# The last three pairs of token tiles: another order of block products for the last pair, and one store DMA per result tile

## The chip, the cores and the metric

The kernel runs on one core of a Trainium2 chip. The core has five engines with a queue of instructions each: TensorE (PE: matrix products, with weight loads beside them), VectorE (DVE), ScalarE (ACT), GpSimd (POOL) and SyncE (SP), which here only issues DMAs. SBUF is the on-chip memory of 128 partitions, PSUM the 128-partition accumulation memory that products are written to. Sixteen DMA engines move data between SBUF and the chip's main memory; they serve queues that SP, ACT and POOL fill. The metric is the device time of one execution in microseconds (us), as the median of several.

## The reference

Attention with normalised queries and keys, then a two-layer network with a PReLU between the layers:

```python
q_n, k_n = rmsnorm(q, g_q), rmsnorm(k, g_k)          # (8, 12, 448, 64)
attn = softmax(q_n @ k_n.T / 8)
x = (attn @ v).transpose(0, 2, 1, 3).reshape(3584, 768)
h = x @ w_in                                         # 768 -> 2048
g = maximum(h, 0) + alpha * minimum(h, 0)
out = g @ w_out                                      # 2048 -> 768, (3584, 768) float32
```

The change concerns only the last line, for the last of the 3584 tokens, and the way in which its results leave the chip.

## The kernel before

The eight batches of 448 tokens are worked through one after the other, attention first, then the two layers. Which product stands where on TensorE is planned in the kernel's text (lists of bursts, gaps and costs), under a manual schedule; the change touches nothing of that plan. Two batches share one buffer of activations, gT: 16 blocks of 128 hidden units by 896 tokens. The 896 tokens are seven tiles of 128.

For most tiles the second layer is `down` (line 500): 16 products of 128 x 384 into one PSUM bank, a copy to an SBUF tile `osb`, and two stores of 64 rows (line 528). The last two batches (b0 = 6) end otherwise. Tile 0 goes through `down`; tiles 1 to 6 go as three pairs (1, 2), (3, 4), (5, 6) through `quad` (line 576), the last work of the kernel. `quad` sees the pair's activations as a 2 x 2 matrix of blocks (tile by half of the 2048 hidden units), and w_out as another (half of the hidden units by half of the 768 columns, OH = 384). It forms the four result blocks with seven block products instead of eight. The sums of blocks that this needs are made beforehand by POOL: `mix_weights` for the weights, `mix` (lines 559 to 566) for the activations, s1 to s4.

Each product is eight matmuls of 128 x 384 (`product`, line 600). In the order of the code: m1 into bank x; m6 into y; m5 into p; m7 into z; m2 added in PSUM onto x; m4 added onto z; m3 added onto p. ACT copies m1 out of x (line 616) and later the finished x (line 627); VectorE forms u2 = y + m1 (619), u3 = z + u2 (624), and the results p + u3 (631), z + u2 (635) and, after m3, p + u2 (640). In the last pair (`last`) m5 and m3 are each split into two halves of 192 columns in banks of their own, so that the final addition and its store go in two pieces.

The banks: x and p are one two-bank tile `oq` (pool pss), y and z a second one; the middle pair takes y and z from the pool psa (`oqa`, one buffer) and x and p from psf (`oqm`, two buffers). The last pair takes its two half-banks for m5 and m3 from psf, so that its own p is not used.

The results go into tiles `osb` of 128 tokens x 384 columns, of which there are four buffers: a new result waits until the store of the one four before it has landed. `send` (line 568) issues the stores. The output is addressed as `out4`, batch, j (0 to 6), 64 rows, 768 columns, where token = row x 7 + j: a tile of 128 tokens is two values of j with 64 rows each, and consecutive rows of one j lie 7 x 768 numbers apart in memory. So a tile is stored by two DMAs of 64 rows of 1536 bytes, both from SP's queue; the two halves of the last result (640) put one of their two DMAs on ACT's queue. In the three pairs that makes 24 DMAs on SP and two on ACT. SP does its issues in order; each waits for the instruction that wrote its source and for the last DMA that used its semaphore.

Of the kernel before, what the change touches and what calls it, by code (L numbers as in the profile page):

```python
# [9 lines left out]
FP32 = mybir.dt.float32  # L10
# [11 lines left out]
def kernel(  # L22
# [12 lines left out]
    nc = tc.nc  # L35
# [4 lines left out]
    J = S // 64  # L40
# [4 lines left out]
    OH = DM // 2  # L45
# [14 lines left out]
    psa = ctx.enter_context(tc.tile_pool(name="psa", bufs=1, space=bass.MemoryType.PSUM))  # L60
# [8 lines left out]
    out4 = out.rearrange("(b p j) m -> b j p m", b=B, j=J)  # L69
# [486 lines left out]
    def block(t, f):  # L556
        return gT[:, ts(f, HF), ts(t, 128)]
# [8 lines left out]
        nc.gpsimd.tensor_sub(out=g[:, 3], in0=block(t, 1), in1=g[:, 1])  # L566

    def send(b0, t, oh, o, c=slice(0, None), split=False):
        for half in range(2):
            bb, j = divmod(2 * t + half, J)  # L570
            dst = out4[b0 + bb, j, :, ts(oh, OH)]
            (nc.scalar if split and half else nc.sync).dma_start(
                out=dst[:, c], in_=o[ds(64 * half, 64), c]
            )

    def quad(b0, t, wide, last=False):

        s1, s2, s3, s4 = (mixes[t][:, n] for n in range(4))
        if wide:
            even, odd = (  # L580
                pss.tile([128, 2, 512], FP32, name="oq", tag="sc") for _ in range(2)
            )
            x, p = even[:, 0], even[:, 1]
        else:
            odd = psa.tile([128, 2, 512], FP32, name="oqa", tag="acc")
            x, p = (psf.tile([128, 512], FP32, name="oqm", tag="mm") for _ in range(2))
        y, z = odd[:, 0], odd[:, 1]
        full = (slice(0, OH),)
        ps = [p]
        if last:  # L590
            full = (slice(0, OH // 2), slice(OH // 2, OH))
            ps = [psf.tile([128, 512], FP32, name="oqm", tag="mm") for _ in range(2)]

        def whole(f, m):
            return lambda ft: w_out_sb[:, HF * f + ft, ts(m, OH)]

        def mixed(n):
            return lambda ft: tw[n, ft // QF][:, ft % QF]

        def product(bank, g, v, first, c=slice(0, OH)):  # L600
            for ft in range(HF):
                nc.tensor.matmul(  # L602
                    out=bank[:, c], lhsT=g[:, ft], rhs=v(ft)[:, c],
                    start=(first and ft == 0), stop=(ft == HF - 1),
                    skip_group_check=True,
                )

        def part(name):
            return ld.tile([128, OH], FP32, name=name, tag="qs", bufs=4)

        def result():
            return ffn.tile([128, OH], FP32, name="osb", tag="osb", bufs=4)

        product(x, block(t, 0), whole(0, 0), True)
        m1 = part("m1")
        nc.scalar.copy(out=m1, in_=x[:, :OH])
        product(y, s2, mixed(1), True)
        u2 = part("u2")
        nc.vector.tensor_add(out=u2, in0=y[:, :OH], in1=m1)
        for b, c in zip(ps, full):  # L620
            product(b, s1, mixed(0), True, c)
        product(z, s3, mixed(2), True)
        u3 = part("u3")
        nc.vector.tensor_add(out=u3, in0=z[:, :OH], in1=u2)
        product(x, block(t, 1), whole(1, 0), False)
        o = result()
        nc.scalar.copy(out=o, in_=x[:, :OH])
        send(b0, t, 0, o)
        o = result()
        for b, c in zip(ps, full):  # L630
            nc.vector.tensor_add(out=o[:, c], in0=b[:, c], in1=u3[:, c])
        send(b0, t + 1, 1, o)
        product(z, block(t + 1, 1), mixed(3), False)
        o = result()
        nc.vector.tensor_add(out=o, in0=z[:, :OH], in1=u2)
        send(b0, t + 1, 0, o)
        o = result()
        for b, c in zip(ps, full):
            product(b, s4, whole(1, 1), False, c)
            nc.vector.tensor_add(out=o[:, c], in0=b[:, c], in1=u2[:, c])  # L640
            send(b0, t, 1, o, c, last)

    def spin(count, wide=True):

# [11 lines left out]
    den_at, av_at, split = {}, {}, {}  # L656
# [5 lines left out]
    while m < NG * J or steps:  # L662
# [21 lines left out]
        while len(bursts[n]) < limit and m < NG * J:  # L684
            y, j = divmod(m, J)
# [91 lines left out]
    for b in range(B - 1):  # L777
# [9 lines left out]
        for n in range(lo, hi):  # L787
            clock += cost(n)
            free = True
            while ups or old or new:  # L790
                two = n in dens and pre(dens[n]) and len(gaps[n]) < 2
                if old and (not ups or (free or two) and (
                    wide(n) or len(old) > sum(wide(c) for c in range(n, hi))
                )):
                    u = old.pop(0)
                elif ups:
                    u = ups.pop(0)
                else:
                    u = new.pop(0)
# [31 lines left out]
    for n, g in enumerate((g_q, g_k)):  # L831
        for h in range(2):
            nc.gpsimd.dma_start(
                out=rows[NF + n : NF + n + 1, ds(64 * h, 64)], in_=g.unsqueeze(0)
# [9 lines left out]
    both, full, lo, hi = slice(0, 2), slice(0, J), slice(0, K0), slice(K0, J)  # L844
    for h in range(2):
        part_square("q", slice(h, h + 1), full, nc.scalar)
    for h in range(2):
# [13 lines left out]
        out=gain, in0=cols[:, NF : NF + 1], in1=cols[:, NF + 1 : NF + 2]  # L861
# [31 lines left out]
    for n in range(NB):  # L893
# [61 lines left out]
        if n in roots:  # L955
            y = roots[n]
# [41 lines left out]
        for k, (f, a) in enumerate(gaps[n]):  # L998
# [3 lines left out]
            else:  # L1002
                f(*a, spare)
                done += 1
                if n in jobs and not (lead and done < 5) and (
                    n < av_at[2 * G - 1] or done % 2
                ):
                    g, c = jobs[n].pop(0)
# [3 lines left out]
                while late and done == late[0][0]:  # L1012
                    _, g, c = late.pop(0)
# [19 lines left out]
    for t in (1, 3, 5):  # L1033
        quad(B - 2, t, t != 3, t == 5)
# [30 lines left out]
```

## Time and profile before

| | us |
|---|---|
| Median of three runs | 426.13 (425.56 to 426.2) |
| The profiled execution, its own time | 425.32 |
| Its span, first to last instruction | 423.6 |
| TensorE busy | 410.0 (97%) |
| Last result written by VectorE (417.83 + 0.36) | 418.19 |
| SP's last eight issues | 415.75 to 420.97 |

The page gives, for each engine, its busy time and its share of the span; the chain that ended last is followed back from the last instruction. A line of a timeline gives start, duration, engine, line of the kernel, operation, and the tile written and read (out<-in); in square brackets the idle time of the engine before it and what ended it. SPq and ACTq are the queues on which these engines issue DMAs: the duration there is that of issuing, and the time from the issue to the landing of the data stands in the answer by source line. A DMA view counts packets (here one per row of 1536 bytes, plus packets of 4 bytes that set the semaphores) and gives the time they took as a share of 16 engines' time in the window. Over the whole span TensorE is busy 97%, and it is the chain's main part (83%).

### The profile page before, as it was taken

To read this page: it belongs to the slowest core of one execution; us is meant where nothing else is said; L and a number is where in the kernel's file an instruction comes from. 1 tells how busy PE (TensorE), PEld (TensorE's weight loads), DVE (VectorE), ACT (ScalarE), POOL (GpSimd) and SP (SyncE) were. 2 spreads that over 40 slices of the span, in tenths; PEclk is the share of its full clock that TensorE was granted. 3 is DMA by queue.
4 is the path that set the end of the run, shared out by engine and by line. 5 is a ranking of instruction groups with operands and counts; after the bars stand their busy time and mean duration, and the time that the engine had idled before them with its cause. 6 is when DMAs were issued, how large, how long until landed. Compare 5 with 4: busy or idle time off the path is not lost.

```text
span 423.6 us, 11137 instructions
## 1 busy us (share of the span) xinstructions
PE 410.0 (97%) x4731; PEld 214.3 (51%) x4731; DVE 224.4 (53%) x335; ACT 278.4 (66%) x390; POOL 290.1 (68%) x201
## 2 busy tenths in 40 slices
PE   8789999999999999999999999999999999999994
PEld 3344454544455454544555445554555545555663
DVE  3875964556464636636565454557463353355232
ACT  5898887778856686668846677667856577255100
POOL 6689994494996289382993569572982999940960
PEclk9999999999999999999999999999999999999998
DMA  8999999999638975568456974547225501100233
GB/s 192 239 244 226 211 192 201 232 163 243 121 82 124 197 126 127 86 135 182 80 117 111 174 177 107 101 85 150 46 44 100 118 2 22 39 19 2 56 85 85
DMA packets 68530, 53.37 MB, mean 126 GB/s; under 512 B 35568, under 2 KB 68480, under 8 KB 68480
## 3 DMA queue, kind: packets, MB, share of 16 engines
q1 hardware_dynamic: 53760, 39.83, 43.0%
q0 software_dynamic: 13984, 11.81, 18.7%
q10 hardware_dynamic: 736, 1.02, 1.0%
q8 instruction: 37, 0.61, 0.6%
q14 instruction: 13, 0.11, 0.1%
HBM read 45.62 MB, written 11.01 MB: 134 GB/s over the span
## 4 chain that ended last, share of the span: by engine, by line
PE 83%; ACT 6%; POOL 4%; DVE 4%; issue 1%; ACTq 1%; POOLq 0%
PE op L508 23%; PE hT L454 21%; PE hTa L454 8%; PE sc L329 8%; PE av L368 5%; PE opa L508 4%; PE oq L602 4%; PE dn L368 3%; ACT expT L343 3%; POOL rden L356 2%; PE avb L368 2%; PE oqm L602 2%; ACT ah L494 2%; PE dnb L389 2%; DVE gT L498 1%
## 5 line engine op out<-in xcount | busy, mean ns | idle before, releaser
L343 ACT ACTIVATE expT<-sc,expb 128x896 f16<-128x896 f32 x168 | 161.3, 1003 | 42.5 <-PE sc L329 42.2
L179 POOL TENSOR_TENSOR qs<-nat,rr 128x896 f16<-128x896 f32 x41 | 68.4, 1690 | 81.8 <-issue 39.3
L454 PE MATMUL hT<-xT,w_in_sb 128*128 128x448 f16 x558 | 115.7, 353 | 0.8 <-DVE gT L498 0.5
L454 PEld LDWEIGHTS <-w_in_sb 128*128 128x128 f16 x768 | 73.2, 98 | 74.0 <-issue 9.4
L508 PE MATMUL op<-w_out_sb,gT 128*128 128x384 f16 x592 | 101.4, 326 | 0.5 <-DVE gT L498 0.5
L508 PEld LDWEIGHTS <-gT 128*128 128x128 f16 x704 | 66.1, 98 | 53.0 <-issue 11.8
L494 ACT ACTIVATE ah<-hT,cols 128x448 f16<-128x448 f32 x92 | 58.1, 632 | 41.8 <-PE hT L454 40.9
L498 DVE TENSOR_TENSOR gT<-hT,ah 128x448 f16<-128x448 f32 x93 | 57.8, 623 | 49.2 <-ACT ah L494 48.4
L155 POOL TENSOR_TENSOR sq<-nat 128x896 f32<-128x896 f32 (+1 forms) x47 | 75.4, 1625 | 8.2 <-DMA nat<-in_q_dram 8.0
L356 POOL TENSOR_TENSOR rden<-rden,expT 128x896 f32<-128x896 f32 x30 | 56.8, 1894 | 2.4
L329 PE MATMUL sc<-qT,kT 64*32 64x448 f16 (+1 forms) x1092 | 53.9, 356 | 4.4 <-ACT expT L343 2.2
L163 DVE TENSOR_REDUCE ss<-sq 128x14 f32<-128x896 f32 (+1 forms) x48 | 48.9, 1038 | 1.5 <-POOL sq L155 1.3
L520 DVE COPY osb<-op 128x384 f32<-128x384 f32 x37 | 20.5, 555 | 54.4 <-PE op L508 54.0
L454 PE MATMUL hTa<-xT,w_in_sb 128*128 128x448 f16 x198 | 42.8, 352 | 0.0
L329 PEld LDWEIGHTS <-kT 64*32 64x32 f16 (+1 forms) x1092 | 16.9, 93 | 35.6 <-issue 29.0
L494 ACT ACTIVATE ah<-hTa,cols 128x448 f16<-128x448 f32 x33 | 20.9, 634 | 15.3 <-PE hTa L454 15.2
L498 DVE TENSOR_TENSOR gT<-hTa,ah 128x448 f16<-128x448 f32 x33 | 20.6, 623 | 17.6 <-ACT ah L494 17.0
L439 DVE TENSOR_TENSOR xT<-av,rden 128x896 f16<-128x896 f32 x16 | 17.5, 1091 | 21.4 <-ACT rden L410 15.4
L368 PEld LDWEIGHTS <-vt 64*32 64x32 f16 (+1 forms) x1260 | 21.4, 94 | 12.7 <-issue 2.5
L368 PE MATMUL av<-expT,vt 64*32 64x448 f16 (+1 forms) x812 | 26.2, 349 | 0.0
L508 PE MATMUL opa<-w_out_sb,gT 128*128 128x384 f16 x112 | 19.4, 327 | 0.0
L563 POOL TENSOR_TENSOR gs<-gT 128x1024 f16<-128x1024 f16 x3 | 6.4, 2117 | 16.6 <-DVE gT L498 16.6
(98 smaller groups left out, 330.5 us busy)
## 6 DMA issues: line engine op xcount, KB each, us to landing
out_dram<-osb SPq DMA_DIRECT2D x110, 96.0 KB, 2.2
nat<-in_q_dram SPq DMA_DIRECT2D x46, 224.0 KB, 4.3
nat<-in_k_dram SPq DMA_DIRECT2D x46, 224.0 KB, 4.6
vt<-in_v_dram POOLq DMA_DIRECT2D x16, 336.0 KB, 6.1
w_in_sb<-in_moe_w_in_dram POOLq DMA_DIRECT2D x12, 256.0 KB, 7.4
w_out_sb<-in_moe_w_out_dram POOLq DMA_DIRECT2D x4, 768.0 KB, 11.3
nat<-in_q_dram ACTq DMA_DIRECT2D x2, 224.0 KB, 4.9
nat<-in_k_dram ACTq DMA_DIRECT2D x2, 224.0 KB, 6.4
```

Source lines behind the costliest of these rows:

```text
L155: nc.gpsimd.tensor_mul(out=sqf[:, c], in0=src[:, c], in1=src[:, c])
L163: nc.vector.tensor_reduce(out=o[:, c], in_=sqs[y, nm][:, c], axis=AXIS_X, op=ALU.add)
L179: eng.tensor_mul(out=t.rearrange("p j h d -> p h j d"), in0=nat[y, nm], in1=rr_t[y][:, "qk".index(nm)].unsqueeze(3).broadcast_to((128, 2, ...
L329: nc.tensor.matmul(out=sc[ds(64 * g + m * c, m), par, :S].rearrange("p (j c) -> p j c", j=J), lhsT=kT[ds(64 * par, 64), j, g, ts(c, m)], r ...
L343: nc.scalar.activation(out=expT[y][:, j], in_=scs[y, j][:, :, :S], func=AF.Exp, scale=QK_SCALE, bias=expb[:, 0:1],)
L356: nc.gpsimd.tensor_add(out=s, in0=e[:, 0] if j == 1 else s, in1=e[:, j])
L368: nc.tensor.matmul(out=accs[g][ds(m * h, m), :S], lhsT=weights(g, y, par, ts(c, m), j), rhs=expT[y][ds(64 * g, 64), j, par, :], start=(j = ...
L454: nc.tensor.matmul(out=hT[:, :S], lhsT=w_in_sb[:, g * G + i, ts(ft, 128)], rhs=xT[b][:, g, i, :], start=(i == 0 and g == 0), stop=(i == G ...
L494: nc.scalar.activation(out=ah, in_=hT[:, :S], func=AF.Copy, scale=alpha_sb[:, ft : ft + 1])
L498: nc.vector.tensor_max(out=gT[:, ft, ds((b & 1) * S, S)], in0=hT[:, :S], in1=ah)
L508: nc.tensor.matmul(out=ops[c][:, :PW], lhsT=gT[:, ft, ts(t, 128)], rhs=w_out_sb[:, ft, ds(oh * OH + c * PW, PW)], start=(ft == 0), stop=(f ...
L602: nc.tensor.matmul(out=bank[:, c], lhsT=g[:, ft], rhs=v(ft)[:, c], start=(first and ft == 0), stop=(ft == HF - 1), skip_group_check=True,)
```

## The change

It has two parts. In `send`, a result tile whose two values of j lie in one batch (j below 6) and that is not the split last one is stored by one DMA of 128 rows: source the 128 partitions of the tile, destination two values of j by 64 rows by 384 columns. Tile 3 has j = 6 of one batch and j = 0 of the next, and stays at two DMAs; so does the split last result. SP's 24 issues become 15: nine of 128 rows, four of 64 rows of 384 columns, two of 64 rows of 192 columns. In `quad`, the steps become functions, and the last pair calls them in the order m1, m6, m2, m7, m5, fourth, m4, m3 instead of m1, m6, m5, m7, m2, fourth, m4, m3, and puts y into a tile of the pool psa, apart from z. The other pairs keep their order and banks. The number and shapes of the instructions on TensorE, VectorE, ACT and POOL stay.

```diff
     def send(b0, t, oh, o, c=slice(0, None), split=False):
+        bb, j = divmod(2 * t, J)
+        if j < J - 1 and not split:
+            nc.sync.dma_start(
+                out=out4[b0 + bb, ds(j, 2), :, ts(oh, OH)][:, :, c],
+                in_=o[:, c],
+            )
+            return
         for half in range(2):
...
-        if wide:
+        full = (slice(0, OH),)
+        if wide or last:
...
         if last:
+            y = psa.tile([128, 2, 512], FP32, name="oqa", tag="acc")[:, 0]
             full = (slice(0, OH // 2), slice(OH // 2, OH))
...
+        def m5():
+            for b, c in zip(ps, full):
+                product(b, s1, mixed(0), True, c)
+
...
+        def m2():
+            product(x, block(t, 1), whole(1, 0), False)
+            o = result()
+            nc.scalar.copy(out=o, in_=x[:, :OH])
+            send(b0, t, 0, o)
+
+        def fourth():
+            o = result()
+            for b, c in zip(ps, full):
+                nc.vector.tensor_add(out=o[:, c], in0=b[:, c], in1=u[3][:, c])
+            send(b0, t + 1, 1, o)
+
...
+        for f in (
+            (m1, m6, m2, m7, m5, fourth, m4, m3) if last
+            else (m1, m6, m5, m7, m2, fourth, m4, m3)
+        ):
+            f()
```

More of the change, by code (lines that the diff above doesn't have):

```diff
@@ L587, in quad @@
         y, z = odd[:, 0], odd[:, 1]
-        full = (slice(0, OH),)
         ps = [p]
         if last:
+            y = psa.tile([128, 2, 512], FP32, name="oqa", tag="acc")[:, 0]
             full = (slice(0, OH // 2), slice(OH // 2, OH))
@@ L612, in result @@
             return ffn.tile([128, OH], FP32, name="osb", tag="osb", bufs=4)
[L614 to L641, printed above, removed]
+        u = {}
+        def m1():
+            product(x, block(t, 0), whole(0, 0), True)
+            u[1] = part("m1")
+            nc.scalar.copy(out=u[1], in_=x[:, :OH])
+        def m6():
+            product(y, s2, mixed(1), True)
+            u[2] = part("u2")
+            nc.vector.tensor_add(out=u[2], in0=y[:, :OH], in1=u[1])
@@ new lines, in m5, with m7 @@
+        def m5():
+            for b, c in zip(ps, full):
+                product(b, s1, mixed(0), True, c)
+        def m7():
+            product(z, s3, mixed(2), True)
+            u[3] = part("u3")
+            nc.vector.tensor_add(out=u[3], in0=z[:, :OH], in1=u[2])
+        def m2():
[8 more added lines that the diff above has]
+            send(b0, t + 1, 1, o)
@@ new lines, in m4, with m3 @@
+        def m4():
+            product(z, block(t + 1, 1), mixed(3), False)
+            o = result()
+            nc.vector.tensor_add(out=o, in0=z[:, :OH], in1=u[2])
+            send(b0, t + 1, 0, o)
+        def m3():
+            o = result()
+            for b, c in zip(ps, full):
+                product(b, s4, whole(1, 1), False, c)
+                nc.vector.tensor_add(out=o[:, c], in0=b[:, c], in1=u[2][:, c])
+                send(b0, t, 1, o, c, last)
+        for f in (
[3 more added lines that the diff above has]
+            f()
```

## The prediction

> **What bounds the kernel now.** The change touches only the last three pairs of token tiles, so I read the end of the span. First the chain of waits from 410 us on:
>
> ```profile
> 412.57 3.90 PE oq L602 x24
> 416.47 1.33 PE oqm L602 x16
> 417.80 0.02 issue
> 417.83 0.36 DVE osb L640
> ```
>
> TensorE works without a gap up to 417.80, and VectorE writes the last result until 418.19. The span is 423.55 (423.6 on the page), so 5.4 us follow in which no engine computes. They belong to the stores. The timeline of the last pair and the timeline of SP alone:
>
> ```profile
> 414.50 0.62 DVE L631 TENSOR_TENSOR osb<-oqm,u 128x192 f32<-128x192 f32 x2
> 415.25 0.48 ACT L627 COPY osb<-oq 128x384 f32<-128x384 f32 x1 [4.79 <-PE oq L602]
> 416.51 0.56 DVE L635 TENSOR_TENSOR osb<-oq,u 128x384 f32<-128x384 f32 x1 [1.39 <-PE oq L602]
> 417.17 0.36 DVE L640 TENSOR_TENSOR osb<-oqm,u 128x192 f32<-128x192 f32 x1
> 417.56 1.19 ACTq L572 DMA_DIRECT2D out_dram<-osb  x2
> 417.83 0.36 DVE L640 TENSOR_TENSOR osb<-oqm,u 128x192 f32<-128x192 f32 x1 [0.30 <-PE oqm L602]
> ```
>
> ```profile
> 415.75 5.22 SPq L572 DMA_DIRECT2D out_dram<-osb  x8
> ```
>
> Eight issues keep SP busy for 5.22 us (0.65 each), to 420.97, while their last source is ready at 418.19: SP is 2.2 us behind. The stores of the last window:
>
> ```profile
> L572 SPq DMA_DIRECT2D out_dram<-osb x2: 551/553/555, 419.8 to 420.4; - x2
> DMA to landing us min/median/max: 1.9/1.9/2.0
> ```
>
> The last issue starts at 420.42 and lands 1.97 later, at 422.39; 1.17 of closing waits follow. So SP's queue of issues sets the end, not a compute engine.
>
> Then what the transfers themselves cost. An ordinary pair of 64-row stores, in two windows of the DMA view (packets, then their time as a share of 16 engines): all of it, and the tail when few engines still work:
>
> ```profile
> DMA packets 160, 0.20 MB, mean 66 GB/s; under 512 B 32, under 2 KB 160, under 8 KB 160
> q1 hardware_dynamic: 160, 0.20, 30.4%
> ```
>
> ```profile
> DMA packets 16, 0.00 MB, mean 33 GB/s; under 512 B 13, under 2 KB 16, under 8 KB 16
> q1 hardware_dynamic: 16, 0.00, 13.9%
> ```
>
> First window, 3 us: 0.304 x 16 x 3000 = 14,590 ns, less 32 semaphore packets at about 9, over 128 rows: 112 ns for a 1536 B row. Second window, 0.14 us: 311 ns less 13 x 9, over 3 rows: 65 ns. So a row costs 112 beside 15 other engines and 65 with few.
>
> Last, the only other 128-row copies on this queue, the q and k loads from 90 us on:
>
> ```profile
> L108 SPq DMA_DIRECT2D nat<-in_q_dram x26: 597/655/1496, 95.1 to 285.4; - x26
> L108 SPq DMA_DIRECT2D nat<-in_k_dram x26: 595/606/1556, 96.9 to 286.8; - x26
> DMA to landing us min/median/max: 3.3/4.2/5.4
> ```
>
> An issue of 128 rows costs SP about 0.60, little more than one of 64 rows (0.47 to 0.60), and lands in as little as 3.3.
>
> **The change, part by part.** Order of products in the last pair: the instructions of TensorE are the same in number and shape; product five (two halves, 1.32) and product two (1.30) change places. y moves to the other accumulation tile; its last reader of pair three ends at 407.94 (L635, 407.39 + 0.56), its first write would come at 409.79, so no wait. x's second product now starts at 411.09; its bank was read by ACT until 410.47. Cost on TensorE 0: the products before it cover each wait; without that cover, x's bank would cost up to the 0.48 of ACT's copy. The ACT copy moves from 415.25 to about 412.6 and its store leaves at 413.1. L631 moves from 414.50 to 415.2, still ahead of the L635 result at 417.07. None of this is on the path unless SP is.
>
> Stores: SP's 24 issues become 15 (pair one 8 to 4, pair three 8 to 6, since tile 3 straddles two batches, last pair 8 to 5; ACT keeps 2). With transfers as quick as now, the last pair's SP issues would start at 413.1, 415.8, 417.08, 417.74, 418.40. The last lands at 418.40 + 1.97 = 420.37, beside ACT's second store at 420.37 (418.22 + 2.15). The gain would be 422.39 - 420.37 = 2.0 us. SP stood still 0.36 beside ACT's first issue (417.51 to 417.87); if that repeats, 1.65.
>
> But the paired store is not just twice a 64-row store. As built, its source is 128 x 384 and its destination 2 x 64 x 384, with the 2 outermost. Every other plain copy on SP's queue has 64 outermost on both sides: the stores are 64 x 384, the loads 64 x 2 x 448. With 2 inside, the loads do spread: two engines with 64 packets each at 65 ns would need 4.2 us plus 1.12 to the first packet and 0.4 to the landing, 5.7, and they land in 3.3. Nothing in the trace shows a copy with 2 outside. So I bound it: 128 rows over 16 engines are 8 x 112 ns = 0.9 us; over two engines 64 x 65 to 64 x 112, 4.2 to 7.2 us. The choice is between rows dealt by the outermost index and rows dealt by number. I take two engines: the pattern that spreads differs from this one exactly in the outermost count. Of the two prices I take 65 ns, the row with few engines active, since the other fourteen are mostly idle.
>
> [...]
>
> The sum with two engines. Their share of SP's queue is 9 paired stores x 64 rows, plus 4 rows from each of four remaining 64-row stores: 592 rows, then 8 half rows at the end. The first row starts 1.12 after the first issue at 397.47, at 398.59. 592 x 0.065 = 38.5, to 437.1; the half rows 0.3; 0.4 to the landing; 1.17 of closing waits: span 438.9. Outside the span lie 425.32 - 423.55 = 1.77: 440.7 for a profiled execution, 15.4 more. The median of the runs, 426.13, is 0.81 above the profiled one: 441.5.
>
> Does this queue ever run dry, so that waits add to it? The result tile (osb) has four buffers, so a result waits for the landing of the store four before it. Stores of pair one end at 402.8, 406.9, 411.1 and 415.2, landing 0.4 later. Results of pair three then come at 406.1, about 407.9, 412.1 and 416.2, the queue still holding rows to 415.2, then to about 424. Those of the last pair follow at about 416.6, 420.9, 425 and 426, ahead of the queue's rows to 437. VectorE stands behind those results, so TensorE will stand too (its two halves of product five wait for a bank read at 416.2), but the engines finish some ten us before the queue. What is late next is the queue alone; the saved issues and the new order are hidden behind it.
>
> **Rivals.** One: 128 rows spread over 16 engines, and SP's backlog goes. For it: loads of 128 rows do spread. Against it: their outermost count is 64. Time 425.32 - 2.0 = 423.3, median 424.1, up to 424.6 with SP's standstill. It decides from about eight engines up: L635's store, issued at 417.08, must land by 420.4, which leaves 1.8 us for its packets, 16 rows at 112.
> Two: two engines at 112 ns. For it: that is what a row mostly takes. Against: it takes it with all engines busy. 592 x 0.047 = 27.8 more: 469.
> Three: the descriptors of the second engine are made only after the first's rows, 128 in a row per store: 9 x 64 x 0.065 = 37 more, 479. The trace neither shows nor excludes it.
> Four: pairing costs nothing and gains nothing because ACT's store and the closing waits set the end anyway. Against it: ACT's store has landed at 420.37, 2.0 before SP's.
>
> **How the numbers follow.** Two engines at about 65 ns 0.60, at up to 112 ns 0.20, one after the other 0.05, spread 0.13, no gain from a spread store 0.02. The predicted time is the first, 441.5. The range goes down to 0.055 a row (435) in case packets overlap and up to 480; what is left out is the spread case and a little beyond, under 2 in 10. By itself the first case holds 436 to 447. A difference of 0.2% (0.85 us) is about what this kernel's measurement can tell from none. Faster 0.13, same 0.01, slower 0.86.
>
> **What will show it.** Right: a DMA share near 2/16 (0.12) with some 45 GB/s from 398 to 437; paired stores landing 5 us or more after issue, each later than the one before; DVE and ACT waiting for out_dram stores; issues of 15 on SP, 0.5 to 0.7 unless the queue is full. Wrong: paired stores that land in 2.6, a last pair with SP idle before its last issue, and a span near 421.6.

## The result, and the profile after

| | before | changed kernel |
|---|---|---|
| median, us | 425.85 (425.3 to 426.2) | 440.63 (440.13 to 441.41) |
| ratio, 95% interval | | 1.035 (1.0328 to 1.0372) |
| the profiled execution, its own time | 425.32 | 440.28 |
| its span | 423.6 | 438.5 |

The change costs 14.8 us. The chain of waits of the changed kernel, from 395 us on (start, duration, what):

```profile
394.99 4.04 PE oq L610 x25
399.02 13.08 DMA out_dram<-osb
412.11 0.03 issue
...
412.20 0.57 DVE osb L658
412.77 0.02 issue
412.79 11.59 DMA out_dram<-osb
424.38 0.03 issue
...
424.47 0.48 DVE osb L658
```

Before, this stretch was products of TensorE alone, up to VectorE's last addition. Now 24.7 us of it are stores of results, and the engines finish at 425.6 while the span ends at 438.5. The waits of the same window (who waited for whom: us in total, times, longest):

```profile
DVE osb L658 <- DMA out_dram<-osb: 6.6, 2, 3.4
DVE osb L652 <- DMA out_dram<-osb: 5.5, 2, 2.8
...
ACT osb L646 <- DMA out_dram<-osb: 4.5, 1, 4.5
...
DVE osb L665 <- DMA out_dram<-osb: 3.4, 1, 3.4
```

and those of SP from 425 us on:

```profile
SPq L1091 <- DMA out_dram<-osb: 6.6, 1, 6.6
```

Six of the eight results that need a buffer again stand for the landing of the store four before them, 2.8 to 4.5 us each, and after the last issue SP waits 6.6 us more for stores to land. The nine paired stores by source line, and what the DMA engines did in a late stretch, 432 to 436 us, when nothing but these stores ran:

```profile
L571 SPq DMA_DIRECT2D out_dram<-osb x9: 540/597/3831, 397.6 to 425.1; - x9
```

```profile
DMA packets 132, 0.20 MB, mean 50 GB/s; under 512 B 2, under 2 KB 132, under 8 KB 132
q1 hardware_dynamic: 132, 0.20, 13.2%
```

An issue takes 0.6 us in the median, as forecast; the longest lasts 3.8, while rows of earlier stores still wait. The transfers are the cost: 13.2% of 16 engines is 2.1 engines. 0.132 x 16 x 4000 ns over 130 rows is 65 ns for a row, and 65 rows per engine in 4 us are one each 61.5 ns, since consecutive rows overlap a little.

### The profile page after: what moved, and what is told of

Read it like the earlier page. It is cut to its first block, busy times and chain, and to the rows that moved or that the text cites. A ratio compares the mean times of both kernels' runs of the same rounds, so it can differ in the third digit from the quotient of the medians.

```text
span 438.5 us, 11126 instructions
## 1 busy us (share of the span) xinstructions
PE 409.8 (93%) x4731; PEld 214.1 (49%) x4731; DVE 224.6 (51%) x335; ACT 278.4 (63%) x390; POOL 290.3 (66%) x201
## 4 chain that ended last, share of the span: by engine, by line
PE 76%; DMA 7%; ACT 5%; POOL 4%; DVE 4%; issue 1%; DVEq 0%; POOLq 0%; ACTq 0%
PE op L508 22%; PE hT L454 21%; PE hTa L454 8%; PE sc L329 8%; DMA out_dram<-osb 6%; PE av L368 4%; PE opa L508 4%; PE dn L368 3%; ACT expT L343 3%; POOL rden L356 2%; PE oq L610 2%; PE avb L368 2%; ACT ah L494 2%; PE dnb L389 2%; DVE gT L498 1%
## 5 line engine op out<-in xcount | busy, mean ns | idle before, releaser
L368 PEld LDWEIGHTS <-vt 64*32 64x32 f16 (+1 forms) x1260 | 21.4, 94 | 12.7 <-issue 2.5
```

The source lines that it names most:

```text
L368: nc.tensor.matmul(out=accs[g][ds(m * h, m), :S], lhsT=weights(g, y, par, ts(c, m), j), rhs=expT[y][ds(64 * g, 64), j, par, :], start=(j = ...
```

## The experiments

The theory: a paired store, whose destination pattern is 2 x 64 rows, runs on two of the sixteen DMA engines, and the rows queued there set the end. Its rivals: the new order or bank costs something; a store of 128 rows is slow in any shape; a fixed loss per store. The part of the span before the last pairs moves by up to 1.0 us between executions (the first of these stores is issued at 397.4 in some profiles and at 398.3 in others), and this blurs the medians. Inside a profile, the tail from the end of VectorE's last addition to the end of the span is free of it; it is 5.4 us before and 12.9 in the changed kernel.

| run | median, us | ratio to before (95%) |
|---|---|---|
| e1, new order, 64-row stores | 424.34 | 0.9966 (0.9953 to 0.998) |
| e2, paired stores, old order | 441.65 | 1.0371 (1.0343 to 1.0399) |
| e3, paired stores as 64 x 2 | 424.31 | 0.9956 (0.9937 to 0.9976) |
| e4, paired stores in the last pair alone | 431.91 | 1.0143 (1.012 to 1.0165) |
| e5, stores of 62 rows | 445.55 | 1.046 (1.0442 to 1.0478) |
| e6, stores of 60 rows | 424.82 | 0.9973 (0.9961 to 0.9986) |
| e7, two queues, old order | 423.83 | 0.9956 (0.9944 to 0.9969) |
| e8, two queues, new order | 424.37 | 0.9957 (0.9945 to 0.9968) |
| e9, stores of 61 rows | 486.15, one execution | |
| e10, every other partition | 425.34, one execution | |

### e1: the new order alone

```diff
-        if j < J - 1 and not split:
+        if False:
```

> Last pair in its new order and tiles, all stores of 64 rows as before (24 issues on SP). Theory (the paired stores run on two DMA engines, and only they cost): SP's last issue moves from 420.4 to about 418.9 to 419.3, since the first result of the last pair is stored 2.6 us earlier; 423.8 to 424.2 against 425.3, 1.1 to 1.5 less, no wait of an engine for a store. Rival (the new order or the bank of y costs part of the 15 us): well above 426, with gaps on TensorE in the last pair.

Measured 424.34, 1.5 below before. The timeline of the last pair:

```profile
413.09 6.56 SPq L579 DMA_DIRECT2D out_dram<-osb  x8
...
417.78 0.36 DVE L665 TENSOR_TENSOR osb<-oqm,u 128x192 f32<-128x192 f32 x1 [0.30 <-PE oqm L610]
```

TensorE ends when it did (the last addition at 417.78, 417.83 before), and SP's eight issues start 2.66 earlier and end at 419.65 instead of 420.97. The last pair's products take 9.15 us from the first to the last in both. The order and the bank of y cost nothing; alone they are a small gain, because a result is stored while SP is free: the tail is 4.1 us instead of 5.4. All of the loss belongs to the paired stores.

### e2: the paired stores alone

```diff
-            (m1, m6, m2, m7, m5, fourth, m4, m3) if last
-            else (m1, m6, m5, m7, m2, fourth, m4, m3)
+            (m1, m6, m5, m7, m2, fourth, m4, m3)
```

(y is again a half of the tile of z.)

> Paired stores alone, order and tiles of the last pair as before. Theory: the queue of two engines sets the end, with the same 592 rows on each, so 440.0 to 440.9 as with both parts, and VectorE waits for stores as there. Rival (the order matters beside them): a difference of more than 1 us from 440.6.

Measured 441.65 (two executions, 440.89 and 442.40) beside 440.63 for both parts. The loss is there without the new order. But 441.65 is above the theory's range and just past the rival's mark of 1 us. In the profiles the tail is 13.7 us here and 12.9 with both parts: the first paired store of the last pair is issued at 422.14 instead of 417.95, and soon after, from 425 to 426, 24 rows move where the changed kernel moves 32. So the old order may cost up to 1 us more beside paired stores; two executions (spans 439.1 and 440.6, against 438.4 to 439.6) do not settle it.

### e3: the same stores with 64 outermost

```diff
-                out=out4[b0 + bb, ds(j, 2), :, ts(oh, OH)][:, :, c],
+                out=out4[b0 + bb, ds(j, 2), :, ts(oh, OH)].rearrange("j p m -> p j m")[:, :, c],
```

> As the changed kernel, but each paired store names its destination as 64 x 2 x 384 instead of 2 x 64 x 384: the same 128 rows, bytes and issues, with 64 outermost. Rows of a tile then land in other places of the same 128, so the output is the reference's with rows exchanged. Theory (the outermost count picks the number of engines): all 16 engines work, paired stores land in about 2.6, SP has no backlog, 423.3 to 424.0. Rival (a store of 128 rows, or of two blocks far apart in memory, is slow on this queue whatever its order): 436 to 441.

Measured 424.31. The nine stores by source line, the DMA view from 397 to 404, in which four of them run, and VectorE's last addition:

```profile
L571 SPq DMA_DIRECT2D out_dram<-osb x9: 539/570/600, 398.3 to 417.9; - x9
...
DMA to landing us min/median/max: 2.2/2.2/2.3
```

```profile
DMA packets 576, 0.79 MB, mean 112 GB/s; under 512 B 64, under 2 KB 576, under 8 KB 576
q1 hardware_dynamic: 576, 0.79, 31.6%
```

```profile
418.64 0.36 DVE L665 TENSOR_TENSOR osb<-oqm,u 128x192 f32<-128x192 f32 x1 [0.30 <-PE oqm L610]
```

Same rows, bytes, issues and memory region; only the order of the two outer counts differs, and 16 us go. The rival that 128 rows, or two blocks of rows, are slow in themselves is out. There is a surprise: 128 rows land in 2.2, no later than 64 rows before. 0.316 x 16 x 7000 ns, less 64 semaphore packets of 9, over 512 rows is 68 ns a row, with all sixteen engines at work (16 semaphore packets a store), where a 64-row store took 112.

The span of this profile is 422.5, so the tail is 3.6 us, 0.5 less than in e1, which stores 64 rows in the same order. Merged with 64 outermost, the stores do save time. The two medians (424.31 and 424.34), blurred by the part before the last pairs, do not show it; the shortest spans of the two, 421.6 and 422.2, do.

### e4: three paired stores

```diff
-        if j < J - 1 and not split:
+        if j < J - 1 and not split and t >= 5:
```

> Paired stores in the last pair alone (three of them), 64 rows elsewhere, new order. Theory (a queue of rows on two engines, 64 rows at 61 ns = 3.9 us per store): issues at 413.1, 415.8, 417.1; rows from 414.2 to 426.0; span 427.8, time 429 to 430, which is 3.7 to 4.7 above before. Rival (a fixed loss per store or per switch, 15 us over nine): 5 above the 423.9 of the order alone, 428.9, but with rows that do not touch end to end.

Measured 431.91, 6.0 above before, 2 more than the theory's range. Three stores of 3.9 would take the rows to 426; they lasted to 427.9. What was missing is a slow start. Packets in three equal windows of 3 us, first the start of this kernel's first paired store and a later stretch of it:

```profile
DMA packets 63, 0.10 MB, mean 34 GB/s; under 512 B 0, under 2 KB 62, under 8 KB 62
```

```profile
DMA packets 99, 0.15 MB, mean 50 GB/s; under 512 B 1, under 2 KB 99, under 8 KB 99
```

(414.2 to 417.2 and 423.8 to 426.8), and the start of the changed kernel's first one (398.8 to 401.8):

```profile
DMA packets 60, 0.09 MB, mean 31 GB/s; under 512 B 0, under 2 KB 60, under 8 KB 60
```

62 rows instead of 98 are 18 fewer per engine, 1.1 us. It happens once, at the first paired store on an idle queue, in both kernels. The DMA share is much the same in the slow window (12.7%) and the later one (13.3%): the two engines are as busy, and a row takes about 98 ns instead of 65. ACT's last two stores run beside these (160 packets on their queue from 418 to 428, 8.7% of 16 engines' time); whether part of the rest is theirs was not tested. So neither a clean 3.9 per store nor a fixed loss, but a queue with a slow start. Why the first rows come slowly stays open.

### e5, e6, e9: the count of rows decides

The kernel before, its 22 whole stores cut to N rows, N = 62, 60, 61:

```diff
-                out=dst[:, c], in_=o[ds(64 * half, 64), c]
+                out=dst[: 64 if split else N, c],
+                in_=o[ds(64 * half, 64 if split else N), c],
```

> The kernel before, its 22 stores of 64 rows in the last three pairs cut to 62 rows; two rows of each are never written, so the output lacks them. Order, issues and everything else as before. Theory (number of engines = the largest up to 16 that divides the outermost counts, 2 for 62): 31 rows on each of two engines, 1.9 us per store, 22 x 31 = 682 rows at 61 ns from 398.6: span 442, time 443 to 445, VectorE waits for stores. Rival (only the 2 x 64 shape of the paired store narrows it): 425.3 or a little less.

> The same with 60 rows, four rows of each store never written. Theory: 60 = 15 x 4, so 15 engines with four rows each: no change, 424.9 to 425.9. Rival (any count that is not 64 or 128 falls to few engines): 430 and more.

> The kernel before, its 22 stores of 64 rows in the last three pairs cut to 61 rows; three rows of each are never written. Theory (the largest number up to 16 that divides the outermost count; 61 is prime, so one engine): 22 x 61 = 1342 rows on one engine at 61 ns, 82 us from 398.7, about 1 us of a slow start: span about 483, time 484 to 487, DMA share 0.06. Rival (any count that does not divide evenly falls to two engines, as 62 did): 22 x 31 rows, 444 to 446.

Measured 445.55, 424.82 and 486.15. The DMA view of 62 rows (405 to 435 us) and of 61 rows (440 to 470):

```profile
q1 hardware_dynamic: 1016, 1.51, 13.4%
```

```profile
q1 hardware_dynamic: 493, 0.74, 6.6%
```

13.4% is 2.1 engines, 6.6% is 1.06. Two rows fewer cost 20 us, three rows fewer 60, four rows fewer nothing; with 60 rows the kernel is even 1.2 faster, and an SP issue takes a median 0.39 us instead of 0.56, for a reason that stays open. The DMA view of 60 rows, from 397 to 405, in which eight stores run:

```profile
DMA packets 600, 0.74 MB, mean 92 GB/s; under 512 B 120, under 2 KB 600, under 8 KB 600
q1 hardware_dynamic: 600, 0.74, 26.8%
```

The 120 packets under 512 B are those that set semaphores: 15 a store, where a store of 64 rows has 16 (128 in eight, shown under e10). Over the last three pairs a store of 62 rows has two (its whole execution has 308 packets under 512 B fewer than before, 14 for each of 22 stores) and one of 61 rows has one (8 beside 485 rows from 440 to 470). So the count of these packets fits the number of engines. The five counts that were run fit one reading, the largest number of engines up to 16 that divides the outermost counts: 62 gives 2 (2.1 by the DMA share), 61 gives 1 (1.06), 60 gives 15 and 64 gives 16 (both by the semaphore packets of a store), and 128 with 2 gives 2 (2.1 in the changed kernel). No other count was run. There is no paired shape in these three, so it is not the pairing as such. All three rivals are out. The range forecast for 62 rows ended 0.6 us below the measured time.

### e7 and e8: the same bottleneck without paired stores

```diff
-            (nc.scalar if split and half else nc.sync).dma_start(
+            (nc.scalar if (split or t >= 5) and half else nc.sync).dma_start(
```

e7 is this in the kernel before, e8 in e1's.

> The kernel before, order and 64-row stores as there; in the last pair the second half of every result goes out on ACT's queue (five issues on SP, five on ACT). Theory (before, SP's queue of eight issues at 0.65 us sets the end): last issues at about 418.3 on both queues, landing at 420.4, 423.3 to 424.1. Rival (the two queues share what makes descriptors, as the 0.36 standstill beside ACT's issue hints): issues slow to 1.2 us a pair, no gain, 425 and more.

> New order and tiles of the last pair, 64-row stores, second halves on ACT's queue in the last pair. Theory: with no backlog on SP the order is worth nothing more, the same 423.3 to 424.1 as with the old order, within 0.4. Rival (issues on two queues slow each other, so spreading them over time by the new order counts): 0.5 to 1.0 below the kernel with the old order.

Measured 423.83 and 424.37. The timeline of e7's last pair:

```profile
415.68 3.29 SPq L572 DMA_DIRECT2D out_dram<-osb  x5
415.69 3.59 ACTq L572 DMA_DIRECT2D out_dram<-osb  x5
...
417.75 0.36 DVE L640 TENSOR_TENSOR osb<-oqm,u 128x192 f32<-128x192 f32 x1 [0.30 <-PE oqm L602]
```

SP is done at 418.97 instead of 420.97. Issues run on the two queues at once with little loss (0.66 and 0.72 each), so the rival falls. With the backlog gone the new order adds nothing that the two intervals show; the medians differ by 0.5 us, the tails (3.8 in e7, 3.6 in e8) by 0.2. e7 beats both kernels: 0.44% under before, 3.8% under the changed kernel.

### e10: rows from every other partition

```diff
-                out=dst[:, c], in_=o[ds(64 * half, 64), c]
+                out=dst[:, c], in_=o[half::2, c]
```

> The kernel before, its 64-row stores taking every other partition of the result tile (even ones, then odd ones) instead of the lower and the upper 64; rows of a tile land in other places of the same 128, so the output is the reference's with rows exchanged. Bytes, issues and shapes stay. [...] Rival (a row takes 120 wherever 16 engines write 64 rows each 21.5 KB apart): rows stay at 112 to 121 and the landing at 2.2.

Measured 425.34 in one execution. The DMA view from 397 to 404 (eight stores of 64 rows), before and in e10:

```profile
DMA packets 640, 0.79 MB, mean 112 GB/s; under 512 B 128, under 2 KB 640, under 8 KB 640
q1 hardware_dynamic: 640, 0.79, 51.8%
```

```profile
q1 hardware_dynamic: 640, 0.79, 32.1%
```

The same 512 rows cost 111 ns each before and 68 in e10, and stores land in a median 2.0 instead of 2.2. So with every other partition the higher price of a row is gone. Why is not shown. e6 speaks for care: its 60 partitions are neighbours too, on 15 engines, and a row costs (0.268 x 16 x 8000 - 120 x 9) / 480 = 69 ns there. Neighbouring partitions alone do not make the price; why 64 of them pay 111 stays open.

## Why the prediction was right

**What bounds the kernel before: right.** SP's eight issues set the end. e7 changes nothing but the queue of three stores, and the kernel gains 0.44%; e1 starts them earlier and gains 0.34%.

**Two engines: right, and it was the step that decided.** It was taken on thin evidence, that every copy that spreads has 64 outermost and this one has 2; that two counts of 2 and 128 give two engines was the author's estimate until the changed kernel showed 2.1. e3 exchanges the two counts and the loss is gone (424.31 us); in plain stores the count of rows does the same, with 62 on 2.1 engines (e5), 61 on 1.06 (e9) and 60 on 15 by the semaphore packets (e6). One store of 128 rows in place of two halves pays with 64 outermost (e3: 15 issues on SP in place of 24, and a tail 0.5 us shorter than with two halves in e1), and as built, with 2 outermost, the change costs 14.8 us.

**65 ns a row: the right number for the wrong reason.** The changed kernel shows 64.8, one row each 61.5. But the forecast called it the price beside few engines, against 112 beside fifteen others. e3 and e10 have all sixteen at work and pay 68: so the number of engines at work is not what raises the price. The same 64 rows cost 111 or 68 by the spacing of their partitions (e10), and 60 neighbours on 15 engines 69 (e6); what makes 111 is not known. That the two engines paid 65 was luck in this step. Rival two rested on the same misreading.

**The sum: right by errors that cancel.** The span was forecast as 438.9 and is 438.5. 592 rows at 61.5 instead of 65 ns take 2.1 less. Against it: the first store's slow start, 1.1, which no step had; the first row at 398.87 in place of 398.59, 0.3; ACT's half rows, which the sum left out, 0.3 by an estimate from SP's eight, which took as long; landing and closing waits 0.1 longer. That makes 438.6. What lies outside the span was 1.78, as before. The median was forecast as 441.5 and is 440.63: 0.4 of this is the span, the rest is that the median lies 0.35 above the profiled execution, where 0.81 was carried over from before.

**The waits: right in kind and place.** The results that wait for a buffer were forecast for about 407.9, 412.1, 416.2 and 416.6, and then 420.9 and 425. In the timeline of the changed kernel VectorE's five start at:

```profile
408.27 0.56 DVE L652 TENSOR_TENSOR osb<-oqm,u 128x384 f32<-128x384 f32 x1 [2.75 <-DMA out_dram<-osb]
...
412.20 0.56 DVE L658 TENSOR_TENSOR osb<-oqa,u 128x384 f32<-128x384 f32 x1 [3.37 <-DMA out_dram<-osb]
...
416.13 0.56 DVE L665 TENSOR_TENSOR osb<-oqm,u 128x384 f32<-128x384 f32 x1 [3.37 <-DMA out_dram<-osb]
...
420.57 0.62 DVE L652 TENSOR_TENSOR osb<-oqm,u 128x192 f32<-128x192 f32 x2 [2.77 <-DMA out_dram<-osb]
...
424.47 0.56 DVE L658 TENSOR_TENSOR osb<-oq,u 128x384 f32<-128x384 f32 x1 [3.27 <-DMA out_dram<-osb]
```

All are within 0.6 us of the forecast, and ACT's is at 416.62. They come 3.9 us (64 rows) apart, and 4.4 where the eight rows of two 64-row stores lie between. One detail was off: TensorE did not stand before product five; it stood before other products, 1.4, 1.2 and 1.5 us. The engines end at 425.6, some 11 us before the queue, so the waits themselves cost nothing, as said.

**The order and the saved issues: right.** The working gave 1.65 to 2.0 for order and issues together, if the stores spread. The tail shows 1.3 for the order alone (e1; 1.5 by the medians) and 1.8 for both (e3). Behind the two engines' queue the saved issues are invisible; e2 leaves open whether the order is.

**The rivals.** One is e3, at 424.31, where it forecast 424.1, up to 424.6: what the change would have been with its two counts exchanged. Three, one engine's rows only after the other's, is excluded by the 2.1 busy engines. Four is excluded by e1 and e7.

## What to carry to other kernels

Before two stores are merged into one, look at the outermost count of both sides of the new pattern: here a 2 and a 62 left 2.1 of the sixteen DMA engines at work and a 61 left 1.06, while stores with 64 outermost had all sixteen (16 semaphore packets each). The issuing engine need not show it: the median issue stayed at 0.6 us in the changed kernel. Read it from the DMA share (one engine is 6%) and from the number of semaphore packets a store leaves (16, 15, 2 or 1 here). When issues are the tail, first try the queue of an idle engine: with three stores moved, e7 gained 1.6 us in the tail, and the larger change, with its stores spread as in e3, 1.8.

## What the runs showed that was not expected

- A row of 1536 bytes costs 111 ns in a store from 64 neighbouring partitions, 68 when the store takes every other partition, 69 with 60 neighbouring partitions, and 68 in the store of 64 x 2 rows, which lands as soon (2.2) as one with half as many rows. Why 64 neighbours pay 111 and 60 do not is not shown; no run here tells an engine from another.
- The first store on two engines moves 60 to 62 rows in its first 3 us, where later ones move 98. Its rows take about 100 ns each instead of 65. No run tells why.
- Behind a narrowed store an SP issue can last as long as a store: a median of 1.8 us with 62 rows (31 rows on an engine at 61 ns are 1.9) and 3.8 with 61 (61 rows are 3.7); in the changed kernel single issues last 2.2 to 4.0. No run tells why.
